# Another start and another written-out order of work in a one-core transformer layer

## The chip, the core and the metric

The kernel runs on one core of a Trainium2 chip. TensorE (PE) does the matrix products out of SBUF into PSUM; VectorE (DVE) and ScalarE (ACT) carry results from PSUM to SBUF and do the element-wise work, GpSimd (POOL) does small statistics, and SyncE (SP) starts most of the transfers (DMAs). ScalarE can start DMAs too. Every engine takes its own instructions strictly in the order in which they were issued. The metric is the device time of one execution in microseconds; of several runs the median counts.

## The reference

A layer of width 448 on 2048 tokens: adaptive layer norm, attention in a sliding window of 8 keys spaced 2 apart, and a multilayer perceptron (MLP) of width 1792. Weights and activations are bf16.

```python
mod = (_silu(c) @ w_mod).reshape(c.shape[0], 6, 1, -1)       # w_mod: 448 x 2688
sa, ca, ga, sb, cb, gb = ...                                 # its six rows
h = _layernorm(x, axis=-1) * (1 + ca) + sa
x = x + ga * attention(h, A_wqkv, A_wo)                      # 16 heads of 28, window 8, dilation 2
h = _layernorm(x, axis=-1) * (1 + cb) + sb
x = x + gb * (silu(h @ B_w1) @ B_w2)
```

So nothing of the attention can be computed before `c`, the first third of `w_mod` (the shift and scale of the first norm) and some tokens are there.

## The kernel before

**Tokens.** The 2048 tokens are cut into four groups (k = 0 to 3) of 512. In a group the even and the odd tokens are kept apart ("par"), since a window of spacing 2 never mixes them. `ld_x` loads a group; group 0 comes as two transfers of 224 KB, each on all 128 partitions, and the others as one of 448 KB each.

**Stages of a group.** `norm1(k)` makes the first norm: statistics per 128 tokens (`Norm`; way "b" is VectorE's `bn_stats`, L453, and `bn_aggr`, L454; way "a" is a sum on ScalarE, L457, a mean on GpSimd, L460, and a sum of squares on ScalarE, L463), the reciprocal root on GpSimd (`rstd`, L465 to 474), and the normalized rows `xn` (L481 on ScalarE or L483 on VectorE). `xn` is transposed, for group 0 by TensorE (`on_pe`, L511) and for the others by DMA transposes on SP's queue (`on_dma`, L533), and then scaled and shifted by the modulation (L518, L520, L538, L540). The string `HOW1` chooses the way of the statistics, a letter for each 128 tokens. `project(k)` multiplies by the query and key weights (L617, 32 matmuls a group in four pieces, each evacuated at L621 by VectorE or ScalarE) and, for each block of 112 queries (`BLOCKS`; nine blocks in all), by the value weights (L641, evacuated at L630). The query and key weights are first copied into a padded layout `wp` (`pads`, L546 to 551).

**Attention** goes by block b and parity: `logits` (L669, then two exponentials on ScalarE, L677, and a mask on VectorE, L701) and `values` (L727, then a reciprocal and a product on VectorE, L732 and 733, and a DMA transpose of the result, L737). `out_proj` (L761) multiplies by `wo` and adds to x (L764). The columns of `wo` and `w2` are multiplied by the gates ga and gb beforehand (L839, L842), which `gate` (L433) makes from `w_mod`; `mod_cols` (L417) makes the shifts and scales.

**MLP.** `ffn1(k)` makes the second norm and the product with `w1` (L788, SiLU on ScalarE, L792); `ffn2(k)` makes the product with `w2` for each 128 tokens (L810), adds x (L815) and stores (L818).

**PSUM.** There are three large tiles ("big": projections, values, logits, MLP) and two small ones ("one": value products, `ps_y`, gates). Two pieces of a projection or one logits step hold two large ones until they are evacuated.

**What sets the order of the work.** `Plan` collects some 720 operations, each with an engine, a planner's cost and what it depends on, but the order of issue is written out by hand: `ORDER` (L43 to 63) lists the operations by their number, that is, by the order in which `P.op` created them; a letter behind the number puts the operation on VectorE (v) or ScalarE (a). `emit` (L195) issues them in that order. The planner's cost of a DMA or its 8 "dma" places do not act on the chip, only the order does. In the trace SP's queue holds about seven transfers at a time: the tenth is issued at 8.68 us, when the third (the 672 KB of `w_mod`) lands.

**The start.** ScalarE's queue issues the table load for SiLU and two small transfers of `c` (L337 to 339). SP's queue issues the two halves of group 0, then `w_mod` columns 0 to 895 (`ld_ma`: one transfer of 672 KB and one of 112 KB), then the query and key weights (112, 224 and 448 KB), group 1, half of the value weights, group 2, the other half, and then the rest (`load`, L334). TensorE runs `WARM` = 6 matmuls on zeros and `JUNK` = 8 pairs of them (L389), which only keep its clock up; two pairs are placed before the product for `c` (L402), two behind it, and four behind the transposes of group 0.

Two weights have rows 384 to 447 left over. They lie in the two halves of 128 partitions and came with one transfer each, whose access pattern is led by a dimension of two: `wqk3` (112 KB, L352) and `w13` (224 KB, L359).

Of the kernel before, what the change touches and what calls it, by code (L numbers as in the profile page):

```python
# [11 lines left out]
ACTF = mybir.ActivationFunctionType  # L12
# [3 lines left out]
D = 448  # L16
H = 16
DH = 28
F = 1792
NF = F // 128  # L20
KT = 4
K3 = D - 384
# [10 lines left out]
CP = 256  # L33
BLOCKS = ((0, 1), (2, 3), (4, 5), (6, 7, 8))
HW = 128 + CP
WARM, JUNK = 6, 8
HOW1 = ("bbbb", "bbbb", "bbbb", "bbbb")
HOW2 = ("ssss", "ssss", "ssss", "ssss")
SEQ = "e0 e1 e2 e3 e4 s0 e5 e6 s1 e7 e8 s2 s3"


ORDER = (
    "3 2 1 57 58 59 68 71 72 80 82 0 4 5 76 69 63 6 7 8 9 10 11 12 17 18 15 16 93 83 84 79 78 62 67 64 92 66 94 98 95a 97 99 101a 86 102 96v 103 100v 104 "  # L43
    "105 13 14 87 89v 107v 88v 90v 91a 23 24 143 147 142 65 60 144 21 22 25 26 19 20 35 36 184 29 30 27 28 31 32 33 34 73 75 77 148 74 81 179 178 106a 61 "
    "149 108 110a 111 109 112a 113 145a 114 116a 117 151a 161a 146v 214 85 150v 215 183 115 152 153 118a 119 154 155 156 120 55 56 121a 180 181v 182v 51 "
    "52 41 42 43 44 39 40 188 189 252 122 123v 160v 158v 159v 128 253 254 281 124 157a 174 282 283 216 70 185 129 255 175a 219 217v 284 176 260 177v 256 "
    "186a 261 262 187a 218v 257 258 259 190 191 192 37 38 47 48 168 169 125v 220 263 170a 171 273 264 221 285 274 172v 173 265 266 193v 275 195a 276 222v "
    "196v 130 162 163 267 268 131 132 133 134 194a 164a 165 166a 167 286 197v 223v 204 205 206a 207 290 277 126 208v 209 291 292 298 299 127a 300 278 287 "
    "224 225 226 227 228 45 46 279 280 288 289 229a 293 269 271 270 272 210 301 311 353 294 312 313 354 233a 355 211v 302 140 303 295 304 296 297 212 198 "
    "199 213a 356 200a 201 319 231v 230v 314 357v 202v 203 315 316 305 306 320 321 232v 322 49 50 340 341 342 343 307 332 358a 333 334 309 308 310 359 361 "  # L50
    "360 362 363a 323 324 325 365 366 317 318 335 344 246 240 336 241 326 327 247v 364v 367 368 369 328 337 345 346 139 242a 243 244a 245 329 330 331 370v "
    "141 371v 373a 372a 338 339 347 348 234 235 236a 237 238a 239 386 349 465 467 387 388 389 392 466 390 391 350 351 352 393 394 248 471 473 53 54 136 "
    "135 138 468 469a 374 376 377 375 249v 137 472 474 470a 378 379 380 381 382 383 476a 384 385 475a 477 478 479 480 481 395 423 402 424 425 396 403 397 "
    "398 483v 452 404 405 399 453 444 484v 426 406 482v 445 454 455 485a 446 409 410 411 431 412 432 433 427 428 413 447 429 430 407 408 504 543 416 456 "
    "417 418 419 420 457 544 545 486 448 487 505 506 488 489 449 458 421 422 450 451 459 460 490 491 492 434 435 436 437 546 438 439 414 415 493 528 494 "
    "495 496 497 498 461 462 500 501 499 463 464 583 502 503 584 585 440 442 441 443 577 579 578 580 586 535 536 537 547 529 530 531 548 514 515 516 517 "
    "532 581v 588v 582v 538 587a 507 518 400 401 550 551 589 590 519 520 533 534 250 556 539 557 558 540 549 251v 559 508 509 564 521 510 591 592 593 595v "
    "522 523 524 565 597a 566 594v 596v 511 598 600 601 541 542 560 567 525 568 569 552 599 561 570 554 553 555 616 602 603 647 649 648 617 618 571 572 "
    "562 563 604 650 606 607 651a 652a 573 575 574 576 653 655 654 656 658v 657v 659 660 661 662 663 665v 512 513 526 527 605 626 619 608 609 610 611 612 "
    "613 614 615 620 627 621 622 664v 623 667v 628 629 640 641 642 643 666a 668 670 671 669 644 674 633 675 634 635 624 625 717 636 637 630 631 632 678 "  # L60
    "679 672 673 676 677 686 680 696 681 687 688 682 683 684 685 689 690 691 692 693 697 698 710 699 711 694 695 645 646 700 701 702 712 713 714 715 716 "
    "638 639 703 704 705 706 718 707 708 709 719 720 "
)


# [9 lines left out]
def half(j):  # L75
    return slice(K3 * j, K3 * j + K3)
# [18 lines left out]
def dram(ap, row, col, dims):  # L95

    w = ap.ap[0][0]
    return bass.AP(ap.tensor, ap.offset + row * w + col, [[r * w + c, n] for r, c, n in dims])
# [118 lines left out]
def layer(ctx, tc, io, safe):  # L217
# [4 lines left out]
    nc = tc.nc  # L222
# [22 lines left out]
    c4 = ct([KT, 128], "c4")  # L245
# [87 lines left out]
    def load(kb, out, in_, after=()):  # L333
        return sp(max(400.0, kb / 0.31), lambda o: nc.sync.dma_start(out=out, in_=in_), [begin] + list(after), 500.0)[0]  # L334


    ld_c = [P.op(("none", 0.0), lambda o: nc.scalar.dma_start(out=c4[0:3, :], in_=c[:, 0:384].rearrange("o (k p) -> (o k) p", p=128))),  # L337
            P.op(("none", 0.0), lambda o: nc.scalar.dma_start(out=c4[3:4, :], in_=c[:, D - 128:D]))]
    ld_c.append(P.op(("none", 3500.0), lambda o: S.preload_act_table(ACTF.Silu)))


    ld_x = [[load(224, x_all[:, 2 * i:2 * i + 2, :].rearrange("p t d -> p (t d)"), x_view[0, :, i, :]) for i in range(2)]]

    def load_mod(c0, c1, after=()):
        kb = (c1 - c0) * 0.75
        return [load(kb, wmod[:, 0:3, c0:c1], rows3(w_mod[:, c0:c1]), after), load(kb / 6, wmod[half(1), 3, c0:c1], w_mod[384:D, c0:c1], after)]

    ld_ma = load_mod(0, 2 * D, [x["deps"][0] for x in ld_x[0]])
    late = [P.op(("sp", 800.0), none, [x["deps"][0] for x in ld_ma])]
    a = load(448, wqk[:, 0:3:2, :], dram(A_wqkv, 0, 0, ((1, 0, 128), (320, 0, 2), (0, 1, 2 * D))), late)  # L350
    b = load(224, wqk[:, 1, :].rearrange("p (a n) -> p a n", a=2), dram(A_wqkv, 128, 0, ((1, 0, 128), (64, D, 2), (0, 1, D))), late)
    ld_qk = [[a], [b], [a], [load(112, wqk3[:], dram(A_wqkv, 128, D, ((128, -D, 2), (1, 0, K3), (0, 1, D))), late)]]  # L352
    ld_v = [load(224, wv[:, 2 * a:2 * a + 2, :], dram(A_wqkv, 192 * a, 2 * D, ((1, 0, 128), (128, 0, 2), (0, 1, D))), late) for a in range(2)]
    ld_x += [[load(448, x_all[:, 4 * k:4 * k + 4, :].rearrange("p (i t) d -> p i (t d)", t=2), x_view[k], late)] * 2 for k in range(1, NC)]
    ld_mo, ld_mb, ld_m2 = load_mod(2 * D, 3 * D, late), load_mod(3 * D, 5 * D, late), load_mod(5 * D, 6 * D, late)
    ld_o = [load(336, wo[:, 0, 0:3, :], rows3(A_wo), late), load(56, wo[half(0), 0, 3, :], A_wo[384:D, :], late)]
    ld_1 = [load(448, w1[:, k, :], B_w1[r:r + 128, :], late) for k, r in ((0, 0), (2, 320))]
    ld_1.append(load(448, w1[:, 1, :].rearrange("p (a n) -> p a n", a=2), dram(B_w1, 128, 0, ((1, 0, 128), (64, F // 2, 2), (0, 1, F // 2))), late))
    ld_1.append(load(224, w13[:], dram(B_w1, 128, F // 2, ((128, -(F // 2), 2), (1, 0, K3), (0, 1, F // 2))), late))  # L359
    ld_2 = [load(112.0 * (f1 - f0), w2[:, f0:f1, :], B_w2[128 * f0:128 * f1, :].rearrange("(f p) d -> p f d", p=128), late) for f0, f1 in ((0, 8), (8, NF))]  # L360


# [78 lines left out]
    class Norm:  # L441
# [55 lines left out]
        def on_pe(self, order, out_of, view, waits, two=False):  # L497

            box, trs = self.box, []


            parts = ((0, 1), (2, 3)) if two else ((0, 1, 2, 3),)

            def tr(o, j):
                if j == 0:
                    for i in range(len(parts)):
                        box[i] = big.tile([128, KT // len(parts), 512], BF16, name="ps_t", tag="big")
                at = slice(128 * order[j], 128 * order[j] + 128)
                for i, ks in enumerate(parts):
                    for k in ks:  # L510
                        T.transpose(box[i][:, k - ks[0], at], box["x"][:, j, 128 * k:128 * k + 128], ident[:])  # L511

            def mod(o, i, ks):
                for k in ks:
                    out_, in_ = out_of(k), view(box[i][:, k - ks[0], :])
                    scale, shift = modc[:, 1, k:k + 1], modc[:, 0, k:k + 1]
                    if o["eng"] == "act":
                        S.activation(out=out_, in_=in_, func=ACTF.Identity, scale=scale, bias=shift)  # L518
                    else:
                        V.tensor_scalar(out=out_, in0=in_, scalar1=scale, scalar2=shift, op0=ALU.mult, op1=ALU.add)  # L520
            for j in range(4):
                trs.append(P.op(("pe", 240.0), lambda o, j=j: tr(o, j), [self.nr[j]] + (trs[-1:] or self.after), take=() if j else ("big",) * len(parts),
                                give=((self.nr[0], "xn"),) if j == 3 else (), mac=213.0))
            self.done = []
            for i, ks in enumerate(parts):
                m = len(ks)
                self.done.append(P.op(either(m * 670.0, m * 455.0), lambda o, i=i, ks=ks: mod(o, i, ks), trs + list(waits) + self.after, give=((trs[0], "big"),)))
            self.trs = trs
# [414 lines left out]
```

## Time and profile before

| | us |
|---|---|
| median of 6 runs | 183.62 (182.35 to 184.92) |
| the profiled execution's own time | 183.61 |
| its span in the trace | 181.8 |
| TensorE busy | 168.4 (93%) |
| ScalarE busy | 115.6 (64%) |
| VectorE busy | 97.0 (53%) |
| first real matmul of group 0's projection | 14.32 |
| first matmul of the MLP | 70.25 |
| last matmul of the MLP ends | about 174.7 |

The difference of 1.8 us between time and span lies around the traced program. The "span in 40 slices" gives a tenth of busy share per digit. In timelines a line is: start, length, engine, line of the kernel, operation, output and inputs, shapes, count, and in brackets how long the engine had been idle and what it waited for. Matmuls overlap, so the length of one says little; the distance between starts is what one costs.

### The profile page before, as it was taken

How to read it: one execution, taken by the hardware profiler on the slowest of the kernel's cores; microseconds unless marked ns; L12 is line 12 of the kernel's file. 1: busy time of each engine (PE TensorE's matmuls, PEld its weight loads, DVE VectorE, ACT ScalarE, POOL GpSimd, SP SyncE). 2: the span in 40 equal slices, each digit the busy share in tenths (PEclk: the TensorE clock that was granted, in tenths of full speed). 3: DMA queues.
4: the chain of work that ended last, by engine and by line, in shares of the span. 5: the costliest groups of instructions: out<-in, count | busy, mean ns of one | idle time of the engine just before them, and what ended most of it. 6: DMA issues, size and time to landing. Idle time of an engine off the chain costs nothing.

```text
span 181.8 us, 3527 instructions
## 1 busy us (share of the span) xinstructions
PE 168.4 (93%) x1401; PEld 77.4 (43%) x1401; DVE 97.0 (53%) x213; ACT 115.6 (64%) x151; POOL 27.7 (15%) x86
## 2 busy tenths in 40 slices
PE   7699989999997999999999999999999999999940
PEld 2163344434534433444455444554434453435510
DVE  7539959987879972630474642669612133021210
ACT  3343999887889678889898545877388612362000
POOL 5603730400240200401000000320020200000000
PEclk9969999999999999999999999999999999999995
DMA  4999499489714437002202121134022310000220
GB/s 137 270 351 316 133 263 99 93 239 161 200 30 125 112 83 214 13 0 61 58 0 54 50 59 48 27 83 112 0 51 60 87 48 0 0 25 4 76 78 14
DMA packets 33283, 17.42 MB, mean 96 GB/s; under 512 B 24236, under 2 KB 32876, under 8 KB 33260
## 3 DMA queue, kind: packets, MB, share of 16 engines
q1 hardware_dynamic: 33252, 17.13, 38.7%
q8 instruction: 13, 0.21, 0.5%
q14 instruction: 10, 0.08, 0.2%
q10 hardware_dynamic: 8, 0.00, 0.0%
HBM read 9.12 MB, written 1.84 MB: 60 GB/s over the span
## 4 chain that ended last, share of the span: by engine, by line
PE 74%; DVE 9%; DMA 6%; ACT 4%; issue 2%; POOL 1%; SPq 1%; ACTq 0%
PE ps_h L788 25%; PE ps_y L810 24%; PE ps_qk L617 9%; PE ps_wo L761 6%; PE ps_v L641 4%; DMA both<-in_w_mod_dram 4%; DVE p L701 2%; DMA oT<-o 2%; PE ps_o L727 2%; ACT p L677 2%; PE ps_l L669 2%; PE ps_w L389 1%; DVE qk L621 1%; PE ps_t L511 1%; POOL rs L469 1%
## 5 line engine op out<-in xcount | busy, mean ns | idle before, releaser
L788 PE MATMUL ps_h<-h,w 128*128 128x512 bf16 (+1 forms) x224 | 47.4, 380 | 0.0
L810 PE MATMUL ps_y<-w,both 128*128 128x448 bf16 x224 | 45.2, 353 | 0.0
L792 ACT ACTIVATE both<-ps_h 128x1024 bf16<-128x1024 f32 x28 | 28.3, 1021 | 25.2 <-PE ps_h L788 25.2
L677 ACT ACTIVATE p<-ps_l 128x896 bf16<-128x896 f32 (+1 forms) x36 | 31.6, 928 | 5.9 <-PE ps_l L669 5.5
L810 PEld LDWEIGHTS <-both 128*128 128x128 bf16 x224 | 21.0, 98 | 20.2 <-issue 0.8
L788 PEld LDWEIGHTS <-w 128*128 128x128 bf16 (+1 forms) x224 | 17.4, 97 | 26.0 <-issue 9.1
L815 DVE TENSOR_TENSOR ot<-ps_y,x_all 128x448 bf16<-128x448 f32 x16 | 9.9, 622 | 26.2 <-PE ps_y L810 26.2
L617 PE MATMUL ps_qk<-h,wp 128*128 128x512 bf16 (+1 forms) x96 | 20.3, 380 | 0.5 <-DVE v L630 0.3
L701 DVE TENSOR_TENSOR p<-p,maskb 128x1792 bf16<-128x1792 bf16 (+1 forms) x18 | 19.8, 1100 | 0.6 <-ACT p L677 0.5
L764 DVE SCALAR_TENSOR_TENSOR x_all<-ps_wo,x_all 128x448 bf16<-128x448 f32 x16 | 9.3, 621 | 15.8 <-PE ps_wo L761 15.8
L617 PEld LDWEIGHTS <-wp 128*128 128x128 bf16 (+1 forms) x128 | 9.5, 97 | 15.8 <-issue 7.4
L621 ACT CAST qk<-ps_qk 128x1024 bf16<-128x1024 f32 x13 | 12.9, 1008 | 4.3 <-PE ps_qk L617 4.3
L460 POOL TENSOR_SCALAR mv<-sums 128x2 f32<-128x2 f32 x8 | 2.9, 364 | 76.0 <-DVE x_all L764 76.0
L481 ACT ACTIVATE xn<-x_all,nm,rs 128x512 bf16<-128x512 bf16 x15 | 12.0, 809 | 2.9 <-POOL nm L472 1.4
L761 PE MATMUL ps_wo<-wo,oT 128*128 128x448 bf16 (+1 forms) x64 | 13.0, 354 | 0.5 <-DMA oT<-o 0.3
L540 DVE TENSOR_SCALAR h<-h,modc 128x512 bf16<-128x512 bf16 x17 | 6.4, 408 | 12.5 <-DMA h<-xn 12.5
L470 POOL TENSOR_TENSOR rs<-rs,negh 128x2 f32<-128x2 f32 x16 | 11.6, 725 | 1.3
L463 ACT ACTIVATE screp<-x_all,mv 128x448 bf16<-128x448 bf16 x16 | 10.6, 665 | 1.7 <-POOL mv L460 1.5
L641 PE MATMUL ps_v<-wv,h 128*128 128x448 bf16 (+1 forms) x56 | 11.0, 354 | 0.6 <-ACT v L630 0.6
L733 DVE TENSOR_TENSOR o<-ps_o,rc 112x448 bf16<-112x448 f32 (+1 forms) x18 | 11.2, 624 | 0.6
L483 DVE TENSOR_SCALAR xn<-x_all,mv,rs 128x512 bf16<-128x512 bf16 x17 | 6.6, 403 | 6.6 <-POOL rs L470 6.6
L727 PE MATMUL ps_o<-v,p 128*128 128x29 bf16 x288 | 9.8, 176 | 0.3 <-DVE p L701 0.3
(81 smaller groups left out, 145.5 us busy)
## 6 DMA issues: line engine op xcount, KB each, us to landing
out_dram<-ot SPq DMA_DIRECT2D x16, 112.0 KB, 1.8
both<-in_w_mod_dram SPq DMA_DIRECT2D x2, 672.0 KB, 7.1
x_all<-in_A_x_dram SPq DMA_DIRECT2D x3, 448.0 KB, 8.0
w<-in_B_w_dram SPq DMA_DIRECT2D x3, 448.0 KB, 3.8
w<-in_B_w_dram SPq DMA_DIRECT2D x1, 896.0 KB, 5.0
both<-in_w_mod_dram SPq DMA_DIRECT2D x2, 336.0 KB
w<-in_B_w_dram SPq DMA_DIRECT2D x1, 672.0 KB
x_all<-in_A_x_dram SPq DMA_DIRECT2D x2, 224.0 KB, 2.7
```

Source lines behind the costliest of these rows:

```text
L470: G.tensor_tensor(out=rs[:, j:j + n], in0=rs[:, j:j + n], in1=negh[:, 0:n], op=ALU.pow)
L481: S.activation(out=out_, in_=in_, func=ACTF.Identity, scale=rs[:, j:j + 1], bias=nm[:, j:j + 1])
L617: T.matmul(ps[:, j, :], lhsT=w.rearrange("p h d -> p (h d)"), rhs=h[rows, :, t, 128:128 + CP], start=start, stop=stop)
L621: return [(either(act_ns(1024), dve_ns(1024)), lambda o, ps: copy_on(o)(out=qk[:, :, g, :, s0:s0 + CP], in_=ps[:].rearrange("p j (t s) -> ...
L641: T.matmul(ps[:, par, 0:D], lhsT=h[rows, par, t, b0:b0 + 128], rhs=wv[rows, t, :], start=(kk == ks[0]), stop=(kk == ks[-1]))
L677: S.activation(out=out_, in_=ps[:, :, 0:4 * nq].rearrange("p j (g q) -> p j g q", q=nq), func=ACTF.Exp, scale=SCALE)
L701: V.tensor_tensor(out=p, in0=p, in1=maskb[:, 1 if b == 0 else 0, 0:nq].unsqueeze(1).to_broadcast([128, H, nq]), op=ALU.mult)
L727: T.matmul(ps[:, h, 0:DH + 1], lhsT=p[:, at:at + 128], rhs=v[:, h, 0:DH + 1], start=True, stop=True)
L761: T.matmul(ps[:, par, 0:D], lhsT=oT[rows, kk, par, s0:s0 + 128], rhs=wo[rows, par, kk, :], start=(q == qs[0]), stop=(q == qs[-1]))
L788: T.matmul(ps[:, j, :], lhsT=w, rhs=h[rows, :, t, :], start=start, stop=stop)
L792: return [(("act", act_ns(1024)), lambda o, ps: S.activation(out=hid[:, k % 2, :, i, :], in_=ps[:], func=ACTF.Silu), after + f2_read.get(k ...
L810: T.matmul(box["ps"][:, 0:D], lhsT=hid[:, k % 2, f % 2, f // 2, 128 * j:128 * j + 128], rhs=w2[:, f // 2 + 7 * (f % 2), :], start=(f == 0) ...
```

## The change

Four things, in the words of the diff:

1. The second half of group 0 is issued by ScalarE's queue, ahead of the two transfers of `c`; the table load for SiLU comes last on that queue. `w_mod` follows the first half directly on SP's queue.
2. `wqk3` and `w13` are each loaded by two transfers of 64 partitions in place of one.
3. `WARM`, `JUNK` go from 6, 8 to 7, 10. `HOW1` of groups 2 and 3 goes from "bbbb" to "bbaa": half of their statistics go from VectorE to ScalarE and GpSimd.
4. `ORDER` is new throughout.

```diff
-WARM, JUNK = 6, 8
-HOW1 = ("bbbb", "bbbb", "bbbb", "bbbb")
+WARM, JUNK = 7, 10
+HOW1 = ("bbbb", "bbbb", "bbaa", "bbaa")
...
-    "3 2 1 57 58 59 68 71 72 80 82 0 4 5 76 69 63 6 7 8 9 10 11 12 17 18 15 16 93 83 84 79 78 62 67 64 92 66 94 98 95a 97 99 101a 86 102 96v 103 100v 104 "
+    "1 7 2 3 4 75 76 80 84 85 79 61 62 63 74 71 0 5 6 8 9 10 11 12 25 26 99 98 100 68 64 104 103 65 105 101v 106v 72 67 88 77 89 90 108 107v 92 93 102a "
...
-    ld_c = [P.op(("none", 0.0), lambda o: nc.scalar.dma_start(out=c4[0:3, :], ...)),
-            P.op(("none", 0.0), lambda o: nc.scalar.dma_start(out=c4[3:4, :], in_=c[:, D - 128:D]))]
-    ld_c.append(P.op(("none", 3500.0), lambda o: S.preload_act_table(ACTF.Silu)))
-    ld_x = [[load(224, x_all[:, 2 * i:2 * i + 2, :].rearrange("p t d -> p (t d)"), x_view[0, :, i, :]) for i in range(2)]]
+    act_q = [P.op(("none", 0.0), lambda o: nc.scalar.dma_start(**first_x(1)))]
+    act_q.append(P.op(("none", 0.0), lambda o: nc.scalar.dma_start(out=c4[0:3, :], ...), act_q[-1:]))
+    act_q.append(P.op(("none", 0.0), lambda o: nc.scalar.dma_start(out=c4[3:4, :], in_=c[:, D - 128:D]), act_q[-1:]))
+    ld_c = [P.op(("none", 4400.0), lambda o: S.preload_act_table(ACTF.Silu), act_q[-1:])]
+    ld_x = [[load(224, **first_x(0)), P.op(("none", 4400.0), none, act_q[:1])]]
...
-    ld_qk = [[a], [b], [a], [load(112, wqk3[:], dram(A_wqkv, 128, D, ((128, -D, 2), (1, 0, K3), (0, 1, D))), late)]]
+    ld_qk = [[a], [b], [a], [load(56, wqk3[half(a), :], A_wqkv[128 * (a + 1):128 * (a + 1) + K3, D * (1 - a):D * (2 - a)], late) for a in range(2)]]
...
-    ld_1.append(load(224, w13[:], dram(B_w1, 128, F // 2, ((128, -(F // 2), 2), (1, 0, K3), (0, 1, F // 2))), late))
+    ld_1 += [load(112, w13[half(a), :], B_w1[128 * (a + 1):128 * (a + 1) + K3, F // 2 * (1 - a):F // 2 * (2 - a)], late) for a in range(2)]
```

The new order, read by its numbers. J is a warm-up matmul, C the product for `c`, M1 and M2 the modulations of the first and second norm, T the transposes of group 0, Q a group's query and key projection (a and b its halves), V, L and A the value projection, logits and value product of a block (e and o are its parities), G the gates, W the output projections, H0 the MLP's first product.

| | TensorE up to the first matmul of the MLP |
|---|---|
| before | J x10, C, J x4, M1, T x4, J x8, Q0, V0, L0e, V1, M2, L1o, G(wo), V2, V3, L0o, A0e, Q1b, L1e, A0o, A1o, Q1a, Q2b, L2e, A1e, G(w2), L2o, W0, V4, L3e, A2e, A2o, V5, Q2a, L3o, A3e, L4o, W1, L4e, A3o, A4o, V6, Q3b with A4e in it, W2, Q3a, H0 |
| after | J x17, C, T, M1, T x3, J x10, V0, V1, Q0, Q1, L0e, G(w2), V2, V3, L0o, M2, L1e, G(wo), A0e, L1o, A0o, Q2b, L2e, A1o, A1e, L2o, V4, W0, Q2a, L3e, A2o, A2e, L3o, V5, V6, L4e, A3o, A3e, L4o, W1, Q3b with V7 and A4o in it, Q3a, W2, A4e, H0 |

| SP's queue | |
|---|---|
| before | x0, x0, `w_mod` 0:2 (two transfers), query and key weights (three), x1, half of wv, x2, half of wv, `w_mod` for the gate of wo, x3, and for M2, then DMA transposes of group 1, half of w2, w13, wo, `w_mod` for the gate of w2 between the transposes of group 2, ... |
| after | x0, `w_mod` 0:2 (two), x1, half of wqk3, half of wv, x2, half of wv, query and key weights (448, 224 KB), half of wqk3, the tail of wo, x3, transposes of group 1 with parts of `w_mod` between them, transposes of group 2 with parts of `w_mod` between them, wo, a third of w1, `w_mod` for the gate of wo, the 672 KB of `w_mod` for M2, two more of w1, the transposes of group 3, ... |

Evacuations of the query and key projections: before 13 on ScalarE and 3 on VectorE, after 6 and 10. The four `pads` are all on VectorE (before three), behind three statistics of group 1, the scaling of half of group 0's h, two more statistics and a normalization. In the MLP the order after puts V8 and the logits of blocks 5, 6 and half of 8 among three of the four second products of group 0, keeps the fourth for behind group 1's first product, and puts the output projections of the last two groups behind that.

## Prediction

> **What bounds the kernel now.** I read the page first (busy times, then the slices), then the busy times by stretch, then TensorE's timeline of the start, its waits from 14 to 70 us, and last VectorE's and SP's timelines there.
>
> ```profile
> PE 168.4 (93%) x1401; PEld 77.4 (43%) x1401; DVE 97.0 (53%) x213; ACT 115.6 (64%) x151; POOL 27.7 (15%) x86
> PE   7699989999997999999999999999999999999940
> ```
> ```profile
> 14.00:70.00 56.00, 52.84 (x570) 24.13 (x568) 48.54 (x103) 45.63 (x59) 13.91 (x35) 1.00 0.71 151
> ```
> ```profile
> 70.00:175.00 105.00, 104.84 (x764) 47.95 (x762) 40.16 (x83) 64.61 (x84) 8.42 (x23) 1.00 0.18 50
> ```
>
> TensorE is the bound. Columns of the stretches are PE, PEld, DVE, ACT, POOL. From 70 to 175 us (the MLP) it idles 105.00 - 104.84 = 0.16 us; from 14 to 70 us (attention) 56.00 - 52.84 = 3.16 us. Its real work is not changed, so the end is: start of real work + that work + idle time. Only the start and 3.16 us can be won. VectorE is at 87% and ScalarE at 81% in the attention stretch.
>
> ```profile
> 5.74 1.41 PE L389 MATMUL ps_w<-both 128*128 128x512 bf16 x4
> 8.71 0.23 PE L417 MATMUL ps_m<-scT,both 128*128 128x1 bf16 x3 [1.57 <-DMA both<-in_w_mod_dram]
> 9.44 0.89 PE L417 MATMUL ps_m<-scT,both 128*128 128x1 bf16 x29 [0.50 <-DMA both<-in_w_mod_dram]
> 10.19 1.87 PE L511 MATMUL ps_t<-ident,xn 128*128 128x128 bf16 x16
> 11.85 2.63 PE L389 MATMUL ps_w<-both 128*128 128x512 bf16 x8
> 14.32 6.63 PE L617 MATMUL ps_qk<-h,wp 128*128 128x512 bf16 x32
> ```
> ```profile
> 12.48 0.99 DVE L520 TENSOR_SCALAR h<-ps_t,modc 128x512 bf16<-128x512 bf16 x2
> 13.38 0.69 DVE L548 COPY wp<-wqk 128x896 bf16<-128x896 bf16 x2
> ```
>
> The start waits for w_mod, whose two pieces release L417 at 8.71 and 9.44. Then come transposes, scaling (h complete at 13.47), the last pad (14.07) and eight warm-ups; all end within half a microsecond of 14.32.
>
> ```profile
> PE ps_l L669 <- DVE qk L621: 1.0, 1, 1.0
> PE ps_v L641 <- ACT v L630: 0.6, 1, 0.6
> PE ps_qk L617 <- DVE v L630: 0.3, 1, 0.3
> ```
>
> These waits are single ones, mostly for an evacuation that sat in VectorE's or ScalarE's queue behind other work.
>
> ```profile
> 0.79 0.89 SPq L334 DMA_DIRECT2D x_all<-in_A_x_dram  x2
> 26.34 3.39 SPq L533 DMA_TRANSPOSE wqk<-xn  x1
> 36.03 0.58 SPq L334 DMA_DIRECT2D both<-in_w_mod_dram  x1
> ```
>
> Two issues on SP take 0.89 us. A DMA transpose can hold SP's queue for 3.39 us, and what stands behind it waits.
>
> **The change part by part.**
>
> *The second x transfer on ScalarE.* SP saves one issue, 0.89 / 2 = 0.45 us, ahead of w_mod. Both ends: 0 if the data path was what limited w_mod, 0.45 if the issue was; I take 0.4, since the DMA share in the stretch 0 to 5 us is 0.50. w_mod then lands near 8.3 and 8.9. On ScalarE the two c issues (0.51 + 0.25) come behind x and the table load (1.28) behind those, so SiLU of c starts near 0.8 + 0.5 + 0.8 + 1.3 = 3.4 in place of 3.26. Nothing is behind it before 5.8; w_mod hides it.
>
> *Warm-ups.* Seventeen stand ahead of the product for c, not ten. Their starts lie 0.427 us apart (10 in the 4.4 us from 1.24), so it moves from 5.62 to 1.24 + 17 x 0.427 = 8.5, and the copy of its result (0.16, and 0.2 of hand-over) to 8.9: no later than w_mod, so I take nothing, and up to 0.4 if w_mod is early. Behind the transposes stand ten, not eight: by the last row of this kind (2.63 / 8 = 0.33) 3.3 us, between 2.1 (0.21, as the matmuls of L617 run) and 4.3. One transpose step in four goes ahead of L417 (saves 1.87 / 4 = 0.4). Transposes end at 8.9 + 0.9 + 1.4 = 11.2, warm-ups between 13.3 and 15.4, by 0.33 at 14.5.
>
> The clock granted was 0.50 from 10 to 13 us, after a hole in TensorE's work from 7.15 to 8.7. The Trainium skill, "TensorE: Matmul & The Clock Gate", section "What's actually happening", says that about 3.4 us of steady work release the clock and an idle window of that length takes it back. Seventeen warm-ups leave a shorter hole than fourteen did, so by that rule the ten cost nearer 2.1 us. Then the warm-ups would end at 13.3 and the total below would be lower by 0.4.
>
> *V0 and V1 first.* They need h and wv, not the pads. On VectorE three statistics of group 1 (2.2 us by the starts 14.74, 15.47, 16.20) now stand ahead of half of h (0.99). If group 1, now right behind w_mod, has landed at 10.1, h is done at 10.1 + 2.2 + 1.0 = 13.3; if it lands at 12 as the waits of SP's queue show for before, at 15.2. Start of real work between 13.3 and 15.2; I take 13.7, nearer the early end, as 784 KB fewer are ahead of group 1. Term: 14.3 - 13.7 = **-0.6**. The pads (four, 0.35 each by the two in 0.69) end near 16.5, covered by 2.9 us of V0 and V1 (1.45 + 1.62 in the chain); without that cover they cost up to 0.5.
>
> *wqk3 and w13 in two pieces.* The 112 KB took about 7.4 us from issue to landing, like the 448 KB beside it. The pieces cost one more issue each on SP (0.45), behind bulk loads, on no path. A gain is not counted apart: group 1's landing contains it.
>
> The Trainium skill, "DMA: Bandwidth & Descriptors", section "How many engines (k)", says that a transfer led by a dimension of two uses two engines only. By it these engines would fall behind by some microseconds for all that follows; group 1 would land at the early end and the start term would be -1.0.
>
> *The attention stretch.* Statistics: four bn pairs (0.73 each) leave VectorE, four sums and four squares (0.57 + 0.1 each, row L463) join ScalarE. Seven qk evacuations (1.13 there, 0.92 on ScalarE by starts) go the other way. From h on to the MLP's first scaling VectorE has 49.2 us by starts before and 50.4 after: 3.65 statistics, 3.0 normalizations, 1.3 pads, 5.0 v, 0.3 replication, 0.8 halos, 3.0 scalings, 10.2 qk, 10.3 masks, 7.4 value norms, 1.0 wo, 0.5 gate, 2.2 adds, 1.6 w2, 0.2 rest. ScalarE gets 2 us less. With h at 13.3, VectorE's work ends at 63.7 plus its waits, which were 6.0 us before (its five longest in this stretch); with 4 it meets TensorE, at 13.7 + 52.84 + 1.44 (V7 now stands ahead of the MLP) = 68.0. Two queues without slack cost each other something: between 0 (all waits gone) and 3.16 (as before); I take 1.5, near the middle. Term: 1.5 - 3.16 = **-1.6**.
>
> *The MLP.* Idle was 0.16. After, the logits of five steps stand among three second products, not four: ScalarE needs 7 SiLU (0.93), 4 squares (0.67), 10 exponentials (0.85), two table loads (1.28), two scalings (0.73) = 21.8 us, TensorE beside it 21.4; 0.4 lost. Between W of group 2 and its MLP stand 10.8 us of TensorE's work, before 13.3 (113.5 to 126.8); adds 1.1, mean 0.4, squares 1.4, root 1.3, normalization 0.7, transpose 1.3 + 2.7, scaling 1.0 and hand-overs add up to some 11: 0.5 lost. Ends 0 and 2.5. Term: **+1.0**.
>
> Sum: -0.6 - 1.6 + 1.0 = -1.2. The profiled execution took 183.61 (span 181.8 and 1.8 around it), and the median is 183.62, so no correction: **182.4 us**.
>
> **The rivals.**
>
> *A: all of it is kept.* The early end everywhere: start 13.3 (-1.0), idle 0.4 in attention (-2.8), MLP dense (0): -3.8, 179.8 us. For it: VectorE's total rose by 1.2 us only. Against: no slack is left between VectorE and TensorE.
>
> *B, slower: w_mod for M2 comes late.* Before, it was issued by 13.9, 11 us ahead of its use at 24.8. Now its 672 KB stand on SP's queue behind the transposes of groups 1 and 2, wo, a third of w1 and the gate's piece. On TensorE M2 stands behind V3 and L0o and ahead of everything. It is reached near 35 (13.7 + 2.9 + 6.5 + 6.5, then L0e, G, V2, V3, L0o 5.0). If group 2's normalized rows are ready at 24.3, issues end at 27.5, 1.8 MB at 340 GB/s (the mean of the stretches from 9 to 14 us) take 5.3, and 1.5 is put on for landing, an estimate from x, which took 2.7 in all for 0.2 MB: 34.3, in time. If group 1's transposes come when they did (19.6 to 22.4) and group 2's at 27 to 30 as SP's row at 26.34 shows, M2 waits until 38.5, 3.5 us; all evacuations slip with it. -1.2 + 3.5 + 0.5 = +2.8: 186.4 us. It decides from group 2's rows later than about 25 on.
>
> *C: it does nothing.* Warm-ups end at 14.5 and the idle time of attention stays, the MLP stays dense: 183.6.
>
> **How the numbers follow.** Forecast 0.42, its own range 181.0 to 183.7; A 0.19; B 0.28; C 0.11. One per cent is about what can be told from no change: faster is below 181.8, slower above 185.5. Faster: A 0.19 and 0.14 of the forecast = 0.33. Same: 0.28 of the forecast, 0.09 of C, 0.03 of a mild B = 0.40. Slower: 0.25 of B, 0.02 of C = 0.27. The range leaves out half of A and the worst of B: 180.0 to 186.4.
>
> **What would show it.** L641 first among real matmuls, at 13.3 to 14.3; the first L617 without a wait for a pad; no wait of M2 (the second group of L417) for a DMA; TensorE's idle time to the MLP's first matmul near 1.5 us and behind it near 1. A first L641 after 14.5 with the warm-ups just ended says that the warm-ups bound it, waits of L417 for w_mod near 35 us say B, waits of L669 or L727 for VectorE say that VectorE is the bound. A clock below 1.00 after 15 us would make all of it wrong.

## Result, and the profile after

| | us | ratio to before, 95% interval |
|---|---|---|
| before, median of 80 runs (beside after) | 184.03 (182.35 to 186.4) | |
| after, median of 38 runs | 182.74 (182.22 to 184.25) | 0.9945 [0.9931, 0.9959] |
| after a second time, unaltered (E1) | 182.77 (182.18 to 183.14) | 0.9929 [0.9904, 0.9954] |

The forecast was 182.4. The first profiled execution of after took 183.91, 1.2 us above its median; the one of E1 took 182.78, so E1's trace stands for after below wherever sums are made. Ratios compare the fast runs of each kernel alone, without those more than 1.5% above its fastest; medians take in all runs.

The timeline of TensorE's start, first profile of after (start, length, engine, line, operation, tiles, shapes, count, idle time before it and its releaser; most lines of the code have moved down by two):

```profile
1.24 6.07 PE L391 MATMUL ps_w<-both 128*128 128x512 bf16 x17 [1.24 <-DVE both L289]
7.25 0.17 PE L404 MATMUL ps_c<-ident,sc 4*128 4x4 bf16 x1
7.55 0.40 PE L513 MATMUL ps_t<-ident,xn 128*128 128x128 bf16 x4
7.78 0.94 PE L419 MATMUL ps_m<-scT,both 128*128 128x1 bf16 x32
8.59 0.38 PE L513 MATMUL ps_t<-ident,xn 128*128 128x128 bf16 x4
9.27 0.72 PE L513 MATMUL ps_t<-ident,xn 128*128 128x128 bf16 x8 [0.30 <-DVE xn L485]
9.82 2.32 PE L391 MATMUL ps_w<-both 128*128 128x512 bf16 x10
12.37 3.11 PE L643 MATMUL ps_v<-wv,h 128*128 128x448 bf16 x16 [0.22 <-DVE h L522]
```

L419 (M1) no longer waits for `w_mod`, and the ten warm-ups end before h: V0 starts at 12.37 behind a wait for VectorE's half of h. TensorE's busy time by stretch, E1's profile (columns as in the prediction's first rows), from the first real matmul to the MLP's first and from there on:

```profile
12.33:70.50 58.17, 54.06 (x577) 24.93 (x577) 51.12 (x95) 44.62 (x67) 11.16 (x32) 1.00 0.63 156
70.50:174.00 103.50, 103.50 (x760) 46.73 (x756) 43.30 (x93) 60.73 (x79) 7.85 (x24) 1.00 0.17 43
```

TensorE idles 58.17 - 54.06 = 4.1 us in attention (4.7 in the first profile), against 3.16 before, and not at all in the MLP. So of the 2.0 us that the start gained, attention gave 1.0 back. E1's waits of TensorE between 12 and 76 us (in total, times, longest) name them:

```profile
PE ps_v L643 <- ACT p L679: 1.1, 2, 0.7
PE ps_wo L763 <- DMA oT<-o: 0.8, 1, 0.8
PE ps_o L729 <- DVE gbc L438: 0.6, 1, 0.6
PE ps_o L729 <- DVE p L703: 0.6, 1, 0.6
PE ps_wo L763 <- ACT p L679: 0.4, 1, 0.4
PE ps_l L671 <- DVE qk L623: 0.4, 2, 0.2
```

The old list had one long wait, for a cast on VectorE. The new one is led by waits for exponentials on ScalarE, for a mask, which comes behind them, for a gate and for the transposed output `oT`.

### The profile page after: what moved, and what is told of

Same layout as the page of the kernel before. It is cut to its first block, busy times and chain, and to the rows that moved or that the text cites. A ratio compares the mean times of both kernels' runs of the same rounds, so it can differ in the third digit from the quotient of the medians.

```text
span 182.0 us, 3554 instructions
## 1 busy us (share of the span) xinstructions
PE 168.1 (92%) x1406; PEld 76.5 (42%) x1406; DVE 104.0 (57%) x219; ACT 110.1 (60%) x153; POOL 26.0 (14%) x86
## 4 chain that ended last, share of the span: by engine, by line
PE 69%; DMA 9%; DVE 7%; ACT 7%; POOL 3%; issue 1%; SPq 0%; ACTq 0%; DVEq 0%
PE ps_h L790 25%; PE ps_y L812 24%; PE ps_wo L763 7%; PE ps_qk L619 5%; PE ps_v L643 4%; ACT p L679 4%; DMA oT<-o 2%; PE ps_o L729 2%; PE ps_l L671 2%; DMA x_all<-in_A_x_dram 2%; DVE st L455 2%; ACT xn L483 2%; DMA wqk<-xn 2%; DMA h<-xn 1%; DMA w<-in_B_w_dram 1%
## 5 line engine op out<-in xcount | busy, mean ns | idle before, releaser
L812 PE MATMUL ps_y<-w,both 128*128 128x448 bf16 x224 | 45.9, 353 | 0.0
L679 ACT ACTIVATE p<-ps_l 128x896 bf16<-128x896 f32 (+1 forms) x36 | 30.7, 934 | 2.1 <-PE ps_l L671 1.9
L790 PEld LDWEIGHTS <-w 128*128 128x128 bf16 (+1 forms) x224 | 16.9, 96 | 27.0 <-issue 11.4
L619 PE MATMUL ps_qk<-h,wp 128*128 128x512 bf16 (+1 forms) x96 | 20.0, 381 | 0.3 <-DVE h L542 0.3
L619 PEld LDWEIGHTS <-wp 128*128 128x128 bf16 (+1 forms) x128 | 9.3, 97 | 16.1 <-issue 6.1
L462 POOL TENSOR_SCALAR mv<-sums 128x2 f32<-128x2 f32 x10 | 3.4, 343 | 76.6 <-DVE x_all L766 76.5
L763 PE MATMUL ps_wo<-wo,oT 128*128 128x448 bf16 (+1 forms) x64 | 12.5, 354 | 1.6 <-DMA oT<-o 1.2
L485 DVE TENSOR_SCALAR xn<-x_all,mv,rs 128x512 bf16<-128x512 bf16 x23 | 8.9, 407 | 8.5 <-POOL rs L472 8.4
L623 DVE CAST qk<-ps_qk 128x1024 bf16<-128x1024 f32 x10 | 12.0, 1219 | 0.1
L729 PEld LDWEIGHTS <-p 128*128 128x128 bf16 x288 | 8.8, 96 | 4.1 <-DVE p L703 0.9
L542 DVE TENSOR_SCALAR h<-h,modc 128x512 bf16<-128x512 bf16 x15 | 5.6, 408 | 8.2 <-DMA h<-xn 8.2
```

The source lines that it names most:

```text
L619: T.matmul(ps[:, j, :], lhsT=w.rearrange("p h d -> p (h d)"), rhs=h[rows, :, t, 128:128 + CP], start=start, stop=stop)
L623: return [(either(act_ns(1024), dve_ns(1024)), lambda o, ps: copy_on(o)(out=qk[:, :, g, :, s0:s0 + CP], in_=ps[:].rearrange("p j (t s) -> ...
L679: S.activation(out=out_, in_=ps[:, :, 0:4 * nq].rearrange("p j (g q) -> p j g q", q=nq), func=ACTF.Exp, scale=SCALE)
L729: T.matmul(ps[:, h, 0:DH + 1], lhsT=p[:, at:at + 128], rhs=v[:, h, 0:DH + 1], start=True, stop=True)
L763: T.matmul(ps[:, par, 0:D], lhsT=oT[rows, kk, par, s0:s0 + 128], rhs=wo[rows, par, kk, :], start=(q == qs[0]), stop=(q == qs[-1]))
L790: T.matmul(ps[:, j, :], lhsT=w, rhs=h[rows, :, t, :], start=start, stop=stop)
```

## Experiments

Every kernel was timed beside before on the same chip. The theory after the result was: the loading (parts 1 and 2 of the change) brings the gain, the order gives part of it back; the rival: the order is what gains, the loading is hidden.

### E1: after, unaltered

No edit.

> The changed kernel unaltered, for a second profile. The first profiled execution had a span of 182.0 us where the timed runs lie mostly near 180.8, so about 1.2 us of it should not be typical. Theory: the start of real work (12.4) is steady and the idle time of TensorE between it and the MLP (4.7 us) is what varies, above all the 1.2 us wait of L763 for a transposed block; expected here 3.5 to 4.5 us of idle time and a start at 12.3 to 12.6. Rival: the start varies with the granted clock (12.4 to 13.5) and the idle time stays at 4.7.

Measured 182.77 (table above): start at 12.33, idle 4.1, clock 1.00. The start is the same in two executions; the idle time in attention was 4.7 in one and 4.1 in the other.

### E2: before, with wqk3 and w13 each in two pieces

```diff
-    ld_qk = [[a], [b], [a], [load(112, wqk3[:], ...)]]
+    ld_qk = [[a], [b], [a], [load(56, wqk3[half(a), :], ...) for a in range(2)]]
...
-    ld_1.append(load(224, w13[:], ...))
+    ld_1 += [load(112, w13[half(a), :], ...) for a in range(2)]
```

> The kernel before with one part of the change: wqk3 and w13 by two transfers of 64 partitions each, order otherwise as it was. Theory supply: the start came earlier because transfers land earlier; with the two busy engines relieved the weights and group 1 land 0.5 to 2 us earlier, but w_mod is ahead of them in the queue, so the first real matmul moves by 0 to 0.3 us and the total by -0.2 (0 to -0.5). Rival order: nothing moves, the total stays within 0.2 us, because warm-ups and pads hold the start.

Measured 184.48 (182.46 to 185.46), ratio 1.0003 [0.9949, 1.0058]. By itself the split does nothing that can be told here; the interval doesn't exclude the 0.2 us of the theory.

### E3: before, with half of x and c on ScalarE's queue

```diff
-    ld_c.append(P.op(("none", 3500.0), lambda o: S.preload_act_table(ACTF.Silu)))
-    ld_x = [[load(224, x_all[:, 2 * i:2 * i + 2, :].rearrange("p t d -> p (t d)"), x_view[0, :, i, :]) for i in range(2)]]
+    act_q = [P.op(("none", 0.0), lambda o: nc.scalar.dma_start(**first_x(1)))]
...
+    ld_c = [P.op(("none", 4400.0), lambda o: S.preload_act_table(ACTF.Silu), act_q[-1:])]
+    ld_x = [[load(224, **first_x(0)), P.op(("none", 4400.0), none, act_q[:1])]]
```

> The kernel before with one part of the change: second half of group 0 and c on ScalarE's queue, order otherwise as it was. Theory supply: w_mod is issued 0.45 us earlier and lands 0.4 to 1.0 us earlier (L417 at 7.8 to 8.3 in place of 8.71 and 9.44); the total falls by 0.4 to 0.8. Rival order: w_mod lands earlier, but the first L617 stays at 14.0 to 14.4 behind the pads and warm-ups; the total stays within 0.2 us.

Measured 182.87 (182.18 to 185.1), ratio 0.9955 [0.992, 0.9991]. The first real matmul comes at 13.09 instead of 14.32. The rate of all transfers over the first 15 us in 40 slices of 0.375 us, before and then E3:

```profile
GB/s 0 0 0 0 34 167 273 341 358 186 91 191 186 272 272 335 213 198 256 347 313 277 261 289 311 313 354 375 385 382 373 380 382 382 301 318 215 330 313 265
```
```profile
GB/s 0 0 0 0 19 153 234 392 393 365 382 416 387 388 282 258 234 258 287 325 315 327 318 306 308 349 390 401 382 370 361 394 270 237 220 315 404 394 373 359
```

From the tenth to the thirteenth slice (3.4 to 4.9 us) before moves 186, 91, 191 and 186 GB/s and E3 365 to 416. The hole is there in each profile with both halves of x on SP's queue and in none with one of them on ScalarE's. With it gone, M1 starts at 7.00 without a wait for `w_mod`, instead of 8.71. By the ratio the gain is 0.8 us, the upper end of what was expected.

### E4: before, with both changes of the loading

The edits of E2 and E3 together, in the old order.

> The kernel before with both parts of the loading and the old order. Theory supply: the start falls to 12.8 to 13.5 and the total by 0.8 to 1.3 us, that is, all of the gain without a new order. Rival order: the total falls by less than 0.4 us and the gain of the changed kernel needs V0 and V1 first.

Measured 181.26 (180.84 to 182.59, 4 runs), ratio 0.9864 [0.9805, 0.9923]: below after, with an order that was written for the old loading. The theory held, and the gain, 2.5 us by the ratio, was twice what it said. VectorE's first pad of `wp`, which waits for `wqk` and has half of h behind it in the queue, in before, E3 and E4:

```profile
12.17 0.40 DVE L548 COPY wp<-wqk 128x896 bf16<-128x896 bf16 x1 [1.57 <-DMA wqk<-in_A_wqkv_dram]
```
```profile
11.43 0.40 DVE L550 COPY wp<-wqk 128x896 bf16<-128x896 bf16 x1 [2.43 <-DMA wqk<-in_A_wqkv_dram]
```
```profile
9.86 0.40 DVE L550 COPY wp<-wqk 128x896 bf16<-128x896 bf16 x1 [0.93 <-DMA wqk<-in_A_wqkv_dram]
```

In E3 `w_mod` is early, and VectorE waits longer for `wqk`; only with wqk3 split as well does `wqk` land 1.6 us earlier. The start then goes to 11.79, and TensorE's idle time in attention stays 3.2 us (55.96 - 52.74), as before. Things that end close together hide each other's gain: by the ratios the two changes won 0 and 0.8 us apart and 2.5 together.

The two traces differ in the clock as well. The eight warm-ups ahead of Q0, in E3 and in E4:

```profile
10.29 2.80 PE L391 MATMUL ps_w<-both 128*128 128x512 bf16 x8
```
```profile
10.06 1.89 PE L391 MATMUL ps_w<-both 128*128 128x512 bf16 x8
```

The granted clock was 0.50 from 9 to 12 us in E3 and 1.00 in E4. In E3 the warm-ups end at 13.09, where Q0 starts, and VectorE's last pad at 13.34. So the earlier `wqk` and the faster warm-ups share the 1.3 us between the two starts, and no run separates them.

### E5: the new order with the old loading

After's `ORDER`, `HOW1`, `WARM` and `JUNK`, with before's lines of E2 and E3.

> The new order with the loading of before: both x halves and then w_mod on SP's queue, c on ScalarE's, wqk3 and w13 whole. Theory (the order costs time, the loading brings it): the three statistics of group 1 that stand ahead of h on VectorE now wait for their data (12 us in the profile of before), so the first real matmul comes near 15.2 instead of 14.3, TensorE's idle time from there to the MLP's first matmul is 4 to 5 us instead of 3.2, and the time is 1.5 to 2.5 us above before: 185.5 to 186.5. Rival (the order suits late weights, since V0 and V1 need only wv and half of wqk's scaling work is hidden): no later start than before and the time within 0.4 us of before.

Measured 187.71 (187.45 to 188.19), ratio 1.0213 [1.0171, 1.0254]: 3.7 us slower than before by the medians. The cost was larger than expected and not where it was expected. The start is early, 12.74 (V0 needs neither pads nor `wqk`, and group 1 had landed by 9.96). The loss is 3.1 us at one wait, for a cast that stood on VectorE behind a product with `w2` that had not landed. E9 is made for that.

### E6: after, with h ahead of group 1's statistics

```diff
-WARM, JUNK = 7, 10
+WARM, JUNK = 7, 7
...
+112v
 149 148 153
...
-112v
 154
```

(Words of `ORDER`; the three warm-up pairs left out stood behind the transposes.)

> After, with VectorE's half of h moved ahead of the three statistics of group 1, and four warm-ups instead of ten behind the transposes (they would end at 12.1 otherwise). Theory (VectorE's queue sets the start in the new order): the first real matmul at 11.5 to 11.7 instead of 12.35, set by ScalarE's half of h. If the 0.7 to 0.8 us are kept to the end, 182.0; if group 1's statistics, 1.0 us later, hold the attention back by as much, 182.7 with TensorE's idle time there up by 0.7. Rival (the warm-ups or wv set the start): the start moves by less than 0.2 us.

Measured 183.38 (182.94 to 184.13), ratio 0.9975 [0.9945, 1.0004]: no gain, rather slower than after. The start went to 11.02, further than expected, and the time was paid back at the projections (this view ends at 20 us):

```profile
11.02 3.02 PE L644 MATMUL ps_v<-wv,h 128*128 128x448 bf16 x16
15.34 0.39 PE L620 MATMUL ps_qk<-h,wp 128*128 128x512 bf16 x1 [1.30 <-DVE wp L551]
15.95 4.27 PE L620 MATMUL ps_qk<-h,wp 128*128 128x512 bf16 x20 [0.21 <-DVE wp L551]
```

V0 and V1 are through by 14.0, and the pads, behind the statistics on VectorE, are not. Group 1's projection starts at 22.79 (E1: 22.03), since its statistics came later. In this order Q1 follows Q0 at once, so group 1's chain on VectorE limits what an earlier start is worth.

### E7: after, with group 2's scalings behind the first exponentials

```diff
-205a 168 ... 204a 235a 234a
+168 ... 235a 234a
...
 265 266
+205a 204a
```

> After, with ScalarE's two scalings of group 2 (1.52 us) moved behind the first two exponentials, so that only the two normalizations of group 3 and the table load stand ahead of them. Theory (ScalarE's queue ahead of the first exponential makes TensorE's new waits): the first exponential at 29.1 to 29.8 instead of 31.2, the wait of V3 for the exponential's release (0.7) gone, the first output product W0 and what follows 0.5 to 1.2 us earlier, time 0.6 to 1.2 us below after. Rival (VectorE's masks, casts and value norms or the output transposes behind the bulk transposes hold that stretch): the idle time moves to the next wait and the time stays within 0.3 us of after.

Measured 182.2 (181.28 to 184.2), ratio 0.9901 [0.9869, 0.9933]: below after by 0.5 us by the medians and by 0.8 by the ratios, at the lower end of the 0.6 to 1.2 expected, and the intervals just touch. ScalarE in E1 and then in E7:

```profile
26.97 1.52 ACT L540 ACTIVATE wqk<-wqk,modc 128x512 bf16<-128x512 bf16 x2 [2.20 <-DMA wqk<-xn]
28.40 1.50 ACT L483 ACTIVATE xn<-x_all,nm,rs 128x512 bf16<-128x512 bf16 x2
29.92 1.28 ACT L679 ACT_TABLE_LOAD   x1
31.21 1.94 ACT L679 ACTIVATE p<-ps_l 128x1024 bf16<-128x1024 f32 x2
```
```profile
26.24 1.52 ACT L484 ACTIVATE xn<-x_all,nm,rs 128x512 bf16<-128x512 bf16 x2 [1.47 <-POOL nm L475]
27.78 1.28 ACT L680 ACT_TABLE_LOAD   x1
29.21 1.94 ACT L680 ACTIVATE p<-ps_l 128x1024 bf16<-128x1024 f32 x2
31.03 1.51 ACT L541 ACTIVATE wqk<-wqk,modc 128x512 bf16<-128x512 bf16 x2
...
40.95 0.81 ACT L541 ACTIVATE h<-h,modc 128x512 bf16<-128x512 bf16 x1 [2.22 <-DVE p L704]
41.67 0.99 ACT L624 CAST qk<-ps_qk 128x1024 bf16<-128x1024 f32 x1
```

The first exponential comes at 29.21 instead of 31.21, and V3 no longer waits. But the same engine then stands 2.2 us at a scaling of group 3 with a ready cast behind it, and TensorE waits for the cast:

```profile
42.71 0.37 PE L672 MATMUL ps_l<-qk 28*128 28x112 bf16 x14 [1.43 <-ACT qk L624]
43.01 0.98 PE L730 MATMUL ps_o<-v,p 128*128 128x29 bf16 x32
43.92 0.68 PE L672 MATMUL ps_l<-qk 28*128 28x112 bf16 x16
44.86 2.69 PE L644 MATMUL ps_v<-wv,wqk 128*128 128x448 bf16 x8 [0.25 <-ACT p L680]
```

This profiled execution took 183.72, among E7's longest; E10 takes that wait away.

### E8: both moves together

The edits of E6 and E7.

> The two moves together (h first with four warm-ups, group 2's scalings behind the first exponentials). If both are separate costs of the new order: 1.3 to 2.0 us below after, about 181.0, level with the old order under the new loading. If one chain holds both (group 1's statistics to group 2's transposes), no more than 0.7 below after.

Measured 182.45 (181.71 to 184.7), ratio 0.9917 [0.9886, 0.9947]. The start is 10.98, and the pads cost the same 1.3 us as in E6. The moves do not add up; nothing is gained over E7.

### E9: after, with w13 alone whole again

```diff
-    ld_1 += [load(112, w13[half(a), :], ...) for a in range(2)]
+    ld_1.append(load(224, w13[:], ...))
```

> After, with w13 alone loaded whole again (one transfer led by a dimension of two, where its second piece stood, right ahead of w2 on SP's queue). Theory (such a transfer holds back what shares its engines, here w2, and VectorE meets the multiplication of w2 in its order): VectorE waits 2 to 3 us for w2 near 51 us, the cast of qk behind it comes late, TensorE waits some 3 us for it near 53 us, and the time is 2 to 3.5 us above after: 185 to 186. Rival (the late loading of before as a whole, x and c on SP's queue and ScalarE's, made that wait): no wait for w2 and the time within 0.4 us of after.

Measured 187.3 (186.56 to 187.72), ratio 1.0173 [1.011, 1.0236]: one transfer that is led by a dimension of two costs 4.2 us by the ratios and 4.6 by the medians, most of what E5 lost against after, and more than the 2 to 3.5 expected. The transfers of `w` issued between 40 and 55 us (KB each, us from issue to landing), in E1 and in E9, where the 224 KB of w13 stand ahead of them:

```profile
w<-in_B_w_dram SPq DMA_DIRECT2D x1, 896.0 KB, 5.2
w<-in_B_w_dram SPq DMA_DIRECT2D x1, 672.0 KB, 5.4
```
```profile
w<-in_B_w_dram SPq DMA_DIRECT2D x1, 896.0 KB, 6.2
w<-in_B_w_dram SPq DMA_DIRECT2D x1, 672.0 KB, 9.3
```

The 672 KB, the part of `w2` that VectorE scales first, land 3.9 us later after their issue. VectorE meets their product with the gate in its order and stands; the cast of qk is the next thing behind it, and TensorE waits for that (in E1 0.20 us):

```profile
53.71 1.16 DVE L845 TENSOR_TENSOR w<-w,gbc 128x896 bf16<-128x896 bf16 x2 [3.21 <-DMA w<-in_B_w_dram]
54.79 1.22 DVE L624 CAST qk<-ps_qk 128x1024 bf16<-128x1024 f32 x1
```
```profile
56.06 0.38 PE L672 MATMUL ps_l<-qk 28*128 28x112 bf16 x16 [3.50 <-DVE qk L624]
```

The two value projections behind this wait take 4.9 us instead of E1's 3.2, at a lower clock (last section).

The Trainium skill, "DMA: Bandwidth & Descriptors", section "How many engines (k)", says that a transfer led by a dimension of two uses two engines; the late landing of what was queued behind it agrees with that.

### E10: E7, with group 3's first scaling behind the next two exponentials

```diff
-241a
...
 303 304
+241a
```

> The kernel with group 2's scalings behind the first exponentials, and in addition ScalarE's first scaling of group 3, which there waited 2.2 us for its transposes ahead of a cast of qk, moved behind the next two exponentials of group 1. Theory (in-order waits on ScalarE make TensorE's idle time in the new order): TensorE's wait of 1.4 us for ScalarE's cast of qk near 42 us goes, the time is 0.8 to 1.5 us below that kernel and 1.3 to 2.0 below after: about 181.0. Rival (the waits only move on to VectorE's masks and the output transposes): within 0.4 us of 182.2.

Measured 181.93 (181.51 to 182.58), ratio 0.9891 [0.9831, 0.9951]. The wait of 1.43 is gone, TensorE's idle time in attention is 57.31 - 53.82 = 3.5 us, and the MLP starts at 69.59 (E1: 70.50). Against after's 0.9945 that is some 1.0 us, below the 1.3 to 2.0 expected, and the intervals overlap; against E7 the medians do not tell them apart. In the trace the mechanism is plain; the size of its gain in time is not settled.

### E11: E4 a second time

No edit.

> The order of before with both changes of the loading, unaltered, a second time. Theory (the loading brings the gain, the order gives part of it back): 1.0 to 2.0 us below after, 181.0 to 181.6. Rival (the first four runs were a lucky sample): level with after within 0.5 us.

Measured 181.84 (181.09 to 182.21), ratio 0.9879 [0.9818, 0.9939]. E4 was not a lucky sample. By E4 and E11 the old order with the new loading stands 0.7 to 0.8% below after, 1.2 to 1.5 us by the ratios and 0.9 to 1.5 by the medians, though E11's interval touches after's.

### E12: E11, with one cast ahead of a waiting normalization

```diff
-361v 206v
+206v 361v
```

> The order of before with both changes of the loading, and one move: on VectorE a normalization for the MLP of group 0, which waits 0.9 us for GpSimd near 51 us, goes behind the cast of qk that stood behind it. Theory (work that waits ahead of a ready cast in an in-order queue is paid by TensorE): TensorE's wait of 1.04 us for that cast near 53 us falls to about 0.5, the normalization itself is not missed (ScalarE's half of the same transpose comes 2.5 us later), and the time is 0.3 to 0.6 us below the kernel without the move, 180.8 to 181.4. Rival (the next wait takes the gain): the wait goes and the time stays within 0.2 us.

Measured 182.17 (181.58 to 182.91), ratio 0.9888 [0.9836, 0.9941]: level with E11. The wait fell as expected, first E11, then E12:

```profile
53.78 0.38 PE L671 MATMUL ps_l<-qk 28*128 28x112 bf16 x16 [1.04 <-DVE qk L623]
```
```profile
53.96 0.38 PE L671 MATMUL ps_l<-qk 28*128 28x112 bf16 x16 [0.51 <-DVE qk L623]
```

From the first real matmul to the MLP's first it takes 55.53 us instead of 56.02, but the start was at 12.68 instead of 11.96. `wqk` was early (VectorE's first pad at 9.82, its last ended at 12.08); Q0 came right behind the warm-ups, which ran late since the clock was 0.50 from 9 to 11 us, where it was 1.00 in E11. A gain of half a microsecond cannot be told from such scatter in six runs.

## Why the prediction was right in sum and wrong in its terms

| term | predicted | first profile of after | E1 |
|---|---|---|---|
| start of real work | -0.6 | -1.95 (12.37 - 14.32) | -1.99 |
| idle time in attention | -1.6 | +1.56 (4.72 - 3.16) | +0.95 (4.11 - 3.16) |
| the MLP | +1.0 | +0.2 (0.27 - 0.06) | -0.06 |
| sum | -1.2 | -0.2 | -1.1 |

The sum of E1's column agrees with the spans (180.8 against 181.8) and with the medians (-1.3). The forecast came within 0.4 us because one term was too small and two were too large, not because its steps held: that is luck.

**The start** was mis-sized, and its own "early end", 13.3, was passed. Several steps of it were off. The second x transfer was given 0.4 us for an issue; E3 shows that it closes a hole in the transfers, after which M1 runs 1.7 us earlier. The seventeen warm-ups and the product for `c` were put at 8.5 and came at 7.25 to 7.5. The ten warm-ups were taken at 0.33 us each; they took 0.23, with the clock at 1.00, near the 2.1 us that stood beside the Trainium skill's rule. SiLU of `c` was put at 3.4; `c` landed late behind x, and it ran at 6.13 in E1. The seventeen warm-ups hide that; the ten of the old order need not, and TensorE waits 1.51 us for it in E11. And the step that no term held: in before, half of h stood on VectorE behind a pad that waited 1.57 us for `wqk`. The new order takes that away (E5 starts at 12.74 with the old loading), and the split of wqk3, which was given no gain of its own, takes it away in the old order (E4).

The clock is a part of the start that the experiments did not separate. With the old order and the old loading it was 0.50 from 10 to 13 us, over the transposes and most of the eight warm-ups; in after, and in E5 with the old loading, the seventeen warm-ups end at 7.3 to 7.6 and it was 1.00 throughout the start. The mean clock of an execution, in the median of the runs that the ratios compare, was 0.983 in before, 0.982 in E2, and 0.991 to 0.993 in E3, E4, E11 and after. As an estimate from these, a mean lower by 0.010 over 181 us is 3.6 us more at 0.50, which costs at most 1.8 us of work at 1.00, warm-ups included.

**V0 and V1 first, and the pads in their cover** were right: h was complete at 12.8 (13.3 said), the pads at 15.6, and the first L619 did not wait for a pad. E6 shows that this cover was only just enough.

**The attention stretch** is the step that failed: "with 4 it meets TensorE", the idle time then put at 1.5. VectorE's sum was a fair account (50.4 us said; it was busy for 51.1 in E1's stretch), but idle time isn't made by the sum of an engine's work; it is made by what stands ahead of a ready instruction. Four scalings and normalizations (3.0 us, begun after a wait of 2.2 us for a transpose) and a table load stood ahead of the first exponential on ScalarE, the engine that was held to win 2 us. E7 moves two of them and the first exponential comes 2.0 us earlier; E10 takes the next such wait away and the idle time falls to 3.5.

**The MLP** lost 0.0 to 0.2 us, not 1.0: all three things that were counted as lost found cover.

**The rivals.** A (all kept, 179.8) fails on the attention stretch. B (`w_mod` for M2 late) did not come: M2 starts at 34.16 in E1, no wait. Its estimate of the landing, 34.3, was close all the same: in E7, which reaches M2 earlier, M2 waits 0.4 us for that transfer, to 33.95. C fails: the warm-ups end at 12.1, and the time is below before by more than its interval.

**What the change does, then.** The loading is worth 2.2 to 2.5 us in the old order (by the ratios of E4 and E11, 0.9864 and 0.9879) and 5 us in the new one (187.7 to 182.7, E5); the order, with `HOW1` and the warm-ups, costs 3.7 us with the old loading and 0.9 to 1.5 with the new. The change is a gain only as a whole or as its loading parts alone. The fastest kernels here, E4 with E11, E10 and E12, lie at 0.986 to 0.989 of before and cannot be told apart.

Left open: why the transfers sink to 91 GB/s near 4 us with both halves of x on SP's queue, what the whole `wqk3` alone would cost in the new order, what `w13` alone is worth in the old one, and what `HOW1` and the warm-ups do apart from the order. None was tried.

## What to carry to other kernels

A weight transfer whose access pattern is led by a dimension of two can be paid by whatever is queued behind it (E9), and an in-order engine passes the delay on to work that needs none of that data; look for the first instruction behind it, not at the transfer's size. When two waits end within a microsecond of each other, test their removal together, since either alone can show little. Read the clock with each such wait. Predict an idle time from the order of each queue, naming what stands ahead of each ready cast or exponential, and not from the sums of busy time.

## What was not expected of the hardware

A short wait can cost clock, and need not. In E7 TensorE waited 1.43 us ahead of 42.71, among small matmuls; the granted clock by 2 us:

```profile
42.00:44.00 2.00, 1.29 (x48) 1.17 (x48) 1.05 (x1) 1.57 (x3) 0.00 (x0) 0.94 0.58 125
44.00:46.00 2.00, 1.75 (x20) 0.90 (x21) 1.91 (x5) 2.00 (x3) 0.00 (x0) 0.50 0.60 135
46.00:48.00 2.00, 2.00 (x9) 0.64 (x8) 1.08 (x2) 0.83 (x2) 0.00 (x0) 0.70 1.50 322
```

The clock (third number from the right) falls to 0.50 after the wait, and V4's eight matmuls take 2.69 us instead of the 1.60 of E1: the wait cost about 1.1 us more than itself. The same follows the 3.50 us in E9 (0.50 from 58 to 60 us), and in E12 a wait of 1.42 us for `c` ahead of 6.77 (0.50 from 9 to 11 us). But the wait of 1.51 us at the same place in E11 left the clock at 1.00, and so did those of 1.30 us at the pads in E6 and E8 and one of 1.21 us in the first profile of after. The Trainium skill, "TensorE: Matmul & The Clock Gate", section "What's actually happening", puts the loss behind an idle window of about 3.4 us; here holes of 1.4 us were enough in two executions, and one of 1.5 us was not in a third. What decides between them no run here shows.
